# First stage of a spectral GFNet and GEGLU kernel: half of the column table mirrored, angles and statistics moved between engines

## The chip, the cores and the metric

One Trainium2 chip, one core. The metric is the device time of one execution in microseconds (us), median of the runs shown. The engines of the core are TensorE (PE, matrix products; PEld is its weight load), VectorE (DVE), ScalarE (ACT), GpSimd (POOL) and SyncE (SP, whose queue issues DMA transfers). Each engine takes its instructions in the order in which the program lists them and waits where a semaphore is not yet there.

## The reference

Batch 1, S = 2048 rows, D = 576 columns, F = 4608, bf16 inputs:

```python
X = rfft2(layernorm(x).astype(f32), axes=(-2, -1))
y = irfft2(X * (w_r + 1j * w_i), s=(S, D), axes=(-2, -1)).astype(bf16)
h = x + y
h2 = h + (gelu(layernorm(h) @ w_gate) * (layernorm(h) @ w_up)) @ w_down
```

`layernorm` has no weights, `eps` is 1e-5, `gelu` is the tanh form.

## The kernel before

The kernel has two halves: the spectral half (two-dimensional transform, product with the filter, inverse transform), which ends at about 68 us, and the gated feed-forward half, which takes the rest. Nothing in the second half is touched.

**Tiling.** The 2048 rows lie as 128 partitions by 16 tiles h: row 16p + h is in partition p, tile h, in `h_sb`. The row transform is split: first a transform of length 16 over groups of partitions (`row16`, a product with the table `F16`), then the column transform with the table `DT` (`f2`), then the twiddles with the table `TF` (`f3`), the filter (`wmul`), and the inverse with the turned twiddle table `TI` (`i3`) and the turned column table `DQ` (`inv_cols`).

**The first stage** is all that is written between lines 174 and 451, an order laid out by hand: there is no scheduler, each engine gets its instructions in the order of the text. It does this:

- The tables. POOL makes index patterns with `iota` and the rounding of the column phases (`kd`, lines 198 and 199); DVE makes the phases (`phases`, line 268) and drops their sign for the cosine (`drop_sign`, line 223); ACT evaluates the sines of the column table `DT` (`col_sin`, line 347, once for sine, once for cosine, 3 x 290 = 870 elements each). The last slice of the table, `D3`, is copied by DVE into the zeroed `DF` (lines 429 and 430).
- The twiddles `TF`: nine orders k of 128 angles. DVE computes the angle (`angle_a`, line 236), brings it into range (`angle_b`, lines 246 and 247) and drops its sign (`angle_c`, line 223); ACT makes the sine (line 253) and cosine (line 256); DVE negates the sine (`minus_sine`, line 259). This is done for two orders first (`first`), ahead of norms(4,8), and for the seven others (`rest`) after the row transform. `turn_tf` (line 262) has SP issue a transposing transfer of TF into TI, once for `first`, once for `rest`.
- Statistics. Nine tiles by DVE (`sd`, which calls `ln_dve`: two bn_stats and an aggregate, lines 116 to 118), seven by ACT (`ln_act`, line 123: tiles 1, 3, 5, 7, 9, 11, 13), whose sums POOL completes (`ln_fin`). POOL takes the power -0.5 for four tiles at a time (`ln_rstd`, lines 132 and 133).
- `norms(lo, hi)`: DVE normalises a tile (line 136), PE multiplies it (`row16`, line 298, and `row16_rest`, line 311, for the part of the columns that is left over). ACT copies the products from PSUM into `Bt` (`evict`, line 322; `evict4`, line 328, whose last call is on DVE). PSUM has four slots of two banks (`two`), handed out in turn; the next user waits until the slot has been read.
- `fill` (line 286) has PE do products that nobody reads: 14 ahead of tile 0, 8 ahead of tile 8, 5 ahead of tile 12, and 3 ahead of the small product `pt` (line 437), from which ACT makes the table `G16` and its negative (line 445).
- The second halves of the filter tables `WR` and `WI` are mirrored rows: POOL gathers them by an indirect transfer (line 381), SP copies them into place (line 411), POOL halves two columns (line 413).

**The SP queue** behind the loads: WR (copy), WI (copy), first `turn_tf`, thirteen pieces of `DQ` (line 421), second `turn_tf` (issued from the loop below, at i = 2), then the first weights of the feed-forward half (`load_gu`, line 145).

**The second stage** is a software pipeline over eight orders k in the order 1, 2, ..., 7, 0 (lines 668 to 709):

```python
if not last:
    f2(order[i])
    if i != 1: f2_out(order[i])
if i == 0:
    f2(order[0] + 8); angle_c(rest); cosine(rest)
    for r in range(2):
        f2_out(order[0] + 8, V.tensor_copy, slice(r, r + 1))
    minus_sine(rest)
```

`f2` is PE's product with `DT` and `DF` (`pq_ps`, line 479), `f2_out` its copy `pq` (line 490, on ACT, except for the second order's two halves on DVE shown here), `f3` the twiddles (`gh_ps`, lines 496 and 497, copied into `g` at line 518), `sum_of` and `wmul` DVE's sums and filter products (lines 529 to 568), `i3` the inverse (`eo_ps`, line 587). i3 of the third order is the first to read a part of TI that the second `turn_tf` writes.

Of the kernel before, what the change touches and what calls it, by code (L numbers as in the profile page):

```python
# [20 lines left out]
P = 128  # L21
S = 2048
# [7 lines left out]
NFT = F // P  # L30
NR = D // 64
NDT = 5
JW = 58
NW = JP // JW
FQ = 3
# [6 lines left out]
def kernel_body(  # L42
# [23 lines left out]
    def two(name):  # L66
        return psum.tile([P, 2, 512], FP32, name=name, tag="two", bufs=4)
# [115 lines left out]
    iota(kv[:, 0:7], [[1, 7]], 1)  # L183
    iota(kv[:, 7:9], [[8, 2]])
    q16 = tmp("q16", [P, P], FP32)
    iota(q16[:], [[16, P]])
    make_identity(nc, ident[:])
    iD = tmp("iD", [P, 3], FP32)
    iota(iD[:], [[P, 3]], 0, 1)
    iota(iD[64:128, 2:3], [[0, 1]], 2 * P + 64 + 192, 1)  # L190
    iJ = tmp("iJ", [P, JP], FP32)
    iota(iJ[:], [[1, 2], [2, JH]])
    iDs = tmp("iDs", [P, 3], FP32)
    G.tensor_scalar(iDs[:], iD[:], 1.0 / D, None, op0=ALU.mult)
    pd, kd = tmp("pd", [P, 3, JP], FP32), tmp("kd", [P, 3, JP], FP32)
# [16 lines left out]
    ia, s2a, s2p = tmp("ia", [P, 1]), tmp("s2a", [P, 1], FP32), tmp("s2p", [P, 1], FP32)  # L212
    V.tensor_scalar(ia[:], ip[:], 7, None, op0=ALU.bitwise_and)
    V.tensor_scalar(s2a[:], ia[:], 127.0 / 8.0, None, op0=ALU.mult)
    V.scalar_tensor_tensor(s2p[:], ip[:], 0.125, s2a[:], op0=ALU.mult, op1=ALU.add)
    ks = tmp("ks", [P, 9], FP32)
    V.tensor_scalar(ks[:], kv[:], s2p[:, 0:1], None, op0=ALU.mult)
    V.tensor_scalar(iu[:], iu[:], 7, None, op0=ALU.bitwise_and)
    mask = tmp("mask", [P, P], FP32)
    V.tensor_scalar(mask[:], iu[:].rearrange("p c l -> p (c l)"), 0.0, None, op0=ALU.is_equal)  # L220

    def drop_sign(dst, src):
        V.tensor_scalar(
# [10 lines left out]
    def angle_a(sl):  # L234
        n = sl.stop - sl.start
        V.scalar_tensor_tensor(
            pr[:, sl],
            q16[:].unsqueeze(1).to_broadcast([P, n, P]),
            s2p[:, 0:1],
            ks[:, sl].unsqueeze(2).to_broadcast([P, n, P]),  # L240
            op0=ALU.mult,
            op1=ALU.add,
        )

    def angle_b(sl):
        V.tensor_scalar(pr[:, sl], pr[:, sl], 2047, None, op0=ALU.bitwise_and)
# [23 lines left out]
            )  # L270

    def row_table():
        V.tensor_tensor(
            F16[:, 0:2, :],
            fs[:].unsqueeze(1).to_broadcast([P, 2, P]),
            mask[:].unsqueeze(1).to_broadcast([P, 2, P]),
            ALU.mult,
        )
        V.tensor_scalar(F16[:, 2, :], F16[:, 0, :], -1.0, None, op0=ALU.mult)

    ps_f = {}

    def fill(dst, n):

        for _ in range(n):
            T.matmul(dst, lhsT=ident[:], rhs=h_sb[:, 0, 0:512], start=True, stop=True)  # L286

    def row16(h):
        if h % 2 == 0 or h == H - 1:
            ps_f[h] = two("f2t")  # L290
        if h % 4 == 0:
            ps_f["f4", h] = two("f4")
        f2t, b = (ps_f[h], 0) if h in ps_f else (ps_f[h - 1], 1)
        fill(f2t[:, b, :], {0: 14, 8: 8, 12: 5}.get(h, 0))
        x = xn[:, h, :]
        for t in range(2):
            for n, d0 in ((0, t * P), (1, DH + t * P)):
                T.matmul(  # L298
                    f2t[:, b, t * 2 * P : (t + 1) * 2 * P],
                    lhsT=x[:, d0 : d0 + P],  # L300
                    rhs=F16[:, n : n + 2, :],
                    start=(n == 0),
                    stop=(n == 1),
                )
        if h < 12:
            row16_rest(h)

    def row16_rest(h):
        o = (h % 4) * P
# [17 lines left out]
    def evict4(h):  # L327
# [2 lines left out]
            ps_f["f4", h][:, 0].rearrange("p (h c l) -> p h c l", h=4, c=16),  # L330
        )

    def sd(*hs):
        for h in hs:
            ln_dve(mv, h)

    def norms(lo, hi):
        for h in range(lo, hi):
# [1 line left out]
            row16(h)  # L340

    wm = [tmp(n, [P, 8 * J], BF16) for n in ("wm_r", "wm_i")]
    xn_pool = tc.tile_pool(name="xn", bufs=1, side="right")
    xn = xn_pool.__enter__().tile([P, H, D], BF16, name="xn")

    def col_sin(r, src, bias):
        A.activation(  # L347
            DT[:, :, :, r, :],
            src[:].rearrange("p t (a j) -> p t a j", a=2),
            ACT.Sin,  # L350
            bias=bias[:],
            scale=-2.0 * PI / D,
        )

    first, rest = slice(0, 2), slice(2, 9)
    ln_act(1)
    ln_act(3)
    sd(0)
    row_table()
    sd(2)  # L360
    ln_fin(slice(1, 4, 2))
    ln_rstd(rstd, mv, 0, 4)
    sd(4, 6)
    norms(0, 4)
    ln_act(5)
    ln_act(7)
    ln_fin(slice(5, 8, 2))
    ln_rstd(rstd, mv, 4, 8)
    ln_act(9)
    evict(0)  # L370
    ln_act(11)
    evict4(0)
    evict(2)
    angle_a(first)
    angle_b(first)
    angle_c(first)
    sine(first)
    cosine(first)
    norms(4, 8)
    for t, w in zip(wm, (A_w_r, A_w_i)):  # L380
        G.indirect_dma_start(
            out=t[:],
            out_offset=None,
            in_=w.rearrange("(a r) j -> a (r j)", r=8),
            in_offset=bass.IndirectOffsetOnAxis(ap=rev[:, 0:1], axis=0),
        )
    G.memset(DF[:], 0.0)
    ln_fin(slice(9, 12, 2))
    sd(8, 10)
    ln_rstd(rstd, mv, 8, 12)  # L390
    evict(4, 6)
    evict4(4)
    ln_act(13)
    sd(12, 14)
    norms(8, 12)
    sd(15)
    ln_fin(slice(13, 14))
    ln_rstd(rstd, mv, 12, 16)
    for z in Zts:
        G.memset(z[:].rearrange("p a w b j -> p (a w b) j")[:, :, JW:], 0.0)  # L400
    phases()
    drop_sign(kd[:], pd[:])
    evict(8, 10)
    evict4(8)
    col_sin(1, pd, zerob)
    col_sin(0, kd, hpib)
    norms(12, 16)
    minus_sine(first)

    for w, t in ((WR, wm[0]), (WI, wm[1])):  # L410
        nc.sync.dma_start(w[:, 9 : H + 1, 0:J], t[:].rearrange("p (r j) -> p r j", r=8))
    for w in (WR, WI):
        G.tensor_scalar(w[:, :, 0 : J : J - 1], w[:, :, 0 : J : J - 1], 0.5, None, op0=ALU.mult)
    turn_tf(first)
    for r in (1, 0):
        for w in range(1 - r, NW):
            j0, j1 = w * JW, (w + 1) * JW
# [7 lines left out]
    for h in range(12, 16):  # L425
        row16_rest(h)
    evict(12, 14, 15)
    angle_a(rest)
    V.tensor_copy(DF[0:32], D3[0:32])
    V.tensor_copy(DF[96:128], D3[96:128])  # L430
    evict4(12)
    angle_b(rest)
    pt = two("pt")
    fill(pt[:, 1, :], 3)
    for x in range(2):
        for p0 in (0, 64):
# [4 lines left out]
                start=True,  # L441
                stop=True,
            )
    for sign in range(2):
        A.activation(
            G16[:, sign, :, :].rearrange("p x q -> p (x q)"),
            pt[:, 0, 0 : 2 * P],
            ACT.Copy,
            scale=G_SCALE if sign == 0 else -G_SCALE,
        )  # L450
    sine(rest)

    xn_pool.__exit__(None, None, None)
    spw = tc.tile_pool(name="spw", bufs=1)
# [565 lines left out]
```

## Time and profile before

| what | us |
|---|---|
| median of 3 runs | 497.56 (497.55 to 497.57) |
| the profiled execution, its own time | 497.44 |
| its span in the profile | 495.7 |
| PE busy | 487.6 (98%) |
| DVE busy | 224.9 (45%) |
| ACT busy | 161.6 (33%) |
| POOL busy | 29.3 (6%) |
| PE, first product of the second stage (`pq_ps`) starts | 25.2 |
| granted PE clock, in each of the slices | full |

How to read it: the shares are means over the whole span. In the first slices the other engines are as busy as PE or more so: from 8 to 12 us DVE is busy for 3.61 of 4.00 us, ACT for 4.00 and PE for 3.98, of which a part are products that nobody reads. From 28 us on PE is busy without a break. The chain of waits says for each moment what the end hung on; the timelines say what stood in each engine's row.

### The profile page before, as it was taken

Reading aid. Unit: us, or ns where it says so; the run is one execution under the profiler, and the core shown is the slowest. Engines: PE = TensorE matmul, PEld = TensorE weight load, DVE = VectorE, ACT = ScalarE, POOL = GpSimd, SP = SyncE. Lnnn points to the kernel's source line nnn. Section 1 sums busy time; section 2 is a strip of 40 time slices with the busy share of each in tenths; the row PEclk is TensorE's granted clock in tenths of the full one; section 3 lists DMA queues with packets and bytes.
Section 4 is the critical chain, followed back from the end, with each engine's and each line's share of the span. In section 5 each row is a group of like instructions: output and inputs, shape, how many; then the busy total and the mean of one; then the engine's idle time right before and its main releaser. Section 6 shows DMA issues by size and latency. Waiting matters only on the chain.

```text
span 495.7 us, 12763 instructions
## 1 busy us (share of the span) xinstructions
PE 487.6 (98%) x5714; PEld 337.6 (68%) x5716; DVE 224.9 (45%) x443; ACT 161.6 (33%) x289; POOL 29.3 (6%) x78
## 2 busy tenths in 40 slices
PE   6999999999999999999999999999999999999997
PEld 3478789885579965555599855555799655555995
DVE  8999884698632157433311244333221333333111
ACT  8999873322211022323300123223110233232000
POOL 8500010011110001000000000000000000000000
PEclk9999999999999999999999999999999999999999
DMA  8739779969990039988730079977700288870000
GB/s 291 214 52 201 207 148 207 185 107 211 213 210 4 3 84 180 209 166 153 145 73 3 1 177 187 199 153 147 144 3 1 79 156 158 156 149 2 13 15 24
DMA packets 89549, 62.33 MB, mean 126 GB/s; under 512 B 23190, under 2 KB 88086, under 8 KB 89494
## 3 DMA queue, kind: packets, MB, share of 16 engines
q1 hardware_dynamic: 89206, 60.34, 61.5%
q0 software_dynamic: 288, 1.18, 0.8%
q8 instruction: 44, 0.72, 0.7%
q14 instruction: 11, 0.09, 0.1%
HBM read 52.65 MB, written 2.36 MB: 111 GB/s over the span
## 4 chain that ended last, share of the span: by engine, by line
PE 95%; POOL 2%; DVE 1%; ACT 1%; issue 0%; POOLq 0%
PE gu L898 57%; PE acc L941 27%; PE pq_ps L479 2%; PE cs_ps L638 2%; PE acc L960 2%; PE eo_ps L587 2%; PE y_ps L770 1%; PE gh_ps L497 1%; PE gh_ps L496 1%; DVE xn L136 1%; POOL rstd L133 0%; PE f2t L298 0%; ACT DT L347 0%; ACT Bt L322 0%; POOL kd L198 0%
## 5 line engine op out<-in xcount | busy, mean ns | idle before, releaser
L898 PE MATMUL gu<-Bt,wgu 64*128 64x512 bf16 (+1 forms) x2646 | 270.6, 363 | 0.0
L898 PEld LDWEIGHTS <-wgu 64*128 64x128 bf16 x2646 | 151.8, 94 | 115.3 <-issue 0.3
L907 DVE TENSOR_TENSOR P_sb<-g_sb,gu 128x512 bf16<-128x512 f32 (+1 forms) x156 | 100.4, 645 | 140.3 <-ACT g_sb L906 140.3
L906 ACT ACTIVATE g_sb<-gu 128x512 f32<-128x512 f32 (+1 forms) x156 | 88.0, 564 | 193.5 <-PE gu L898 193.5
L941 PEld LDWEIGHTS <-P_sb 64*128 64x128 bf16 x2160 | 122.2, 94 | 10.9
L941 PE MATMUL acc<-wd,P_sb 64*128 64x288 bf16 x1440 | 90.9, 283 | 0.0
L950 DVE TENSOR_TENSOR part<-part,acc 128x576 f32<-128x576 f32 x15 | 11.3, 755 | 112.6 <-ACT part L949 112.6
L949 ACT COPY part<-acc 128x576 f32<-128x576 f32 x15 | 9.6, 640 | 122.8 <-PE acc L941 122.8
L941 PE MATMUL acc<-wd_a,P_sb 64*128 64x288 bf16 x720 | 46.8, 283 | 0.0
L898 PE MATMUL gu<-Bt,wgu_e 64*128 64x256 bf16 (+1 forms) x162 | 12.5, 305 | 0.0
L795 DVE TENSOR_SCALAR hrow<-h_sb,mv,rstd 128x1152 bf16<-128x1152 bf16 x14 | 12.2, 868 | 0.6 <-POOL rstd L833 0.6
L479 PE MATMUL pq_ps<-DT,Bt 128*128 128x290 bf16 x64 | 12.3, 286 | 0.0
L286 PE MATMUL f2t<-h_sb,ident 128*128 128x512 bf16 x26 | 8.3, 473 | 3.9 <-DMA h_sb<-in_A_x_dram 3.9
L133 POOL TENSOR_TENSOR rstd<-rstd,mhalf 128x1 f32<-128x1 f32 (+1 forms) x16 | 11.7, 729 | 1.3
L952 DVE TENSOR_TENSOR h_sb<-h_sb,part 128x576 bf16<-128x576 bf16 x15 | 11.4, 758 | 0.5
L898 PEld LDWEIGHTS <-wgu_e 64*128 64x128 bf16 x162 | 10.4, 94 | 1.1
L479 PEld LDWEIGHTS <-Bt 128*128 128x128 bf16 x96 | 9.2, 97 | 2.5
L132 POOL TENSOR_SCALAR rstd<-mv 128x1 f32<-128x1 f32 (+1 forms) x16 | 4.0, 247 | 116.4 <-DVE mv L118 116.1
L638 PE MATMUL cs_ps<-DQ,EO 58*128 58x290 bf16 x144 | 10.8, 283 | 0.0
L490 ACT CAST pq<-pq_ps 128x580 bf16<-128x580 f32 x15 | 9.9, 663 | 0.2
L298 PE MATMUL f2t<-F,xn 128*128 128x256 bf16 x64 | 9.3, 275 | 0.6 <-DVE xn L136 0.6
L123 ACT ACTIVATE junk<-h_sb 128x576 bf16<-128x576 bf16 x14 | 9.4, 674 | 0.6 <-DMA h_sb<-in_A_x_dram 0.6
(138 smaller groups left out, 280.0 us busy)
## 6 DMA issues: line engine op xcount, KB each, us to landing
wgu<-in_B_w_gate_dram SPq DMA_DIRECT2D x46, 432.0 KB
wgu<-in_B_w_up_dram SPq DMA_DIRECT2D x46, 432.0 KB
wd_a<-in_B_w_down_dram SPq DMA_DIRECT2D x1, 1728.0 KB
wd<-in_B_w_down_dram SPq DMA_DIRECT2D x1, 1728.0 KB
wd<-in_B_w_down_dram SPq DMA_DIRECT2D x6, 288.0 KB
out_dram<-h_sb SPq DMA_DIRECT2D x3, 576.0 KB
h_sb<-in_A_x_dram SPq DMA_DIRECT2D x4, 288.0 KB
h_sb<-in_A_x_dram SPq DMA_DIRECT2D x2, 576.0 KB
```

The costliest lines, as they stand in the source:

```text
L133: G.tensor_tensor(dst[:, sl], dst[:, sl], mhalf[:, sl], ALU.pow)
L479: T.matmul(ps[:, par, 0:JP], lhsT=Bt[:, t, col], rhs=DT[:, t // 2, par] if t < 4 else DF[:, par], start=(t == par), stop=(t == 4),)
L587: T.matmul(pv[:, n], lhsT=z[:, a, w].rearrange("p b j -> p (b j)"), rhs=TI[:, ts[k], 1 - a : 3 - a, :], start=(a == 0), stop=(a == 1),)
L638: T.matmul(ps[:, e, 0:JP], lhsT=EO[x][rows, w, 2 * g : 2 * g + 2].rearrange("p h e k l -> p (h e k l)"), rhs=DQ[rows, w] if w or e else DT ...
L795: V.tensor_scalar(hrow[:], h_sb[:, h, :].rearrange("p (r k) -> p r k", k=64).unsqueeze(2).to_broadcast([P, NR, 2, 64]), mv2[:, h, 0:1], rs ...
L898: T.matmul(gu[:, c, 0:n], lhsT=w[rows, r, i * P : (i + 1) * P], rhs=hl[tcnk % 2][rows, r, lo:hi], start=(r == 0), stop=(r == NR - 1),)
L906: A.activation(g_sb, gu[:, 0, 0:n], ACT.Gelu_apprx_tanh)
L907: V.tensor_tensor(p_sb(f)[:, lo:hi], g_sb, gu[:, 1, 0:n], ALU.mult)
L941: T.matmul(accs[i][:, c, 0:DH], lhsT=p_sb(f)[rows, st * P : (st + 1) * P], rhs=wd[f // NWA][rows, f % NWA, c * DH : (c + 1) * DH], start=( ...
L950: V.tensor_tensor(part, part, accs[1][:, :, 0:DH], ALU.add)
L952: V.tensor_tensor(hv, hv, part, ALU.add)
L960: T.matmul(acc[:, 0, 0:DH], lhsT=p_sb(f)[:, st * P : (st + 1) * P], rhs=wd[f // NWA][:, f % NWA, cc], start=(f == 0), stop=(f == NFT - 1),)
```

## The change

The text of the first stage is rearranged, and some instructions get another form or engine:

- The column table: phases and sines are computed for 73 of the 145 columns of each kind (`JM = 73`), so ACT's two sines have 438 elements each. The others are mirror images with a sign that depends on the partition's parity: a new function `mirror` has DVE write them with four tensor_scalar instructions. The last column of one kind is zeroed by POOL.
- The first two twiddles' angles go to POOL (`first_a`, `first_b`: five instructions), among its statistics; DVE only drops the sign. ACT makes their sines after the last eviction. The other angles keep their form, but `angle_a` and `angle_b` come later in DVE's row, and `angle_c` moves behind the two copies `f2_out(order[0] + 8)`.
- Tile 13's statistics go from ACT to DVE; in `sd` a tile's aggregate is issued between the two bn_stats of the next.
- `gather(1)`, the indirect transfer for WI, is issued by POOL after the last `ln_rstd`; `gather(0)` keeps its place. The memsets of DF, and of the table's last column, follow it.
- The leftover products of four tiles (`rests`) are issued together behind the tiles; fills are 14 ahead of tile 0 and 12 ahead of tile 8, none ahead of tile 12.
- The mask of the row table is folded into one instruction; the negative of `G16` is made by DVE.

Core of the diff:

```diff
-    iJ = tmp("iJ", [P, JP], FP32)
-    iota(iJ[:], [[1, 2], [2, JH]])
+    iJ = tmp("iJ", [P, 2 * JM], FP32)
+    iota(iJ[:], [[1, 2], [2, JM]])
...
+    def first_a():
+        G.tensor_scalar(qs[:, 0], q16[:], s2p[:, 0:1], None, op0=ALU.mult)
+        G.tensor_tensor(
+            prf[:], qs[:].to_broadcast([P, 2, P]), ks[:, 0:2].unsqueeze(2).to_broadcast([P, 2, P]), ALU.add
+        )
+
+    def first_b():
+        G.tensor_scalar(abf[:], prf[:], 1.0 / S, C23, op0=ALU.mult, op1=ALU.add)
+        G.tensor_scalar(abf[:], abf[:], -C23, -float(S), op0=ALU.add, op1=ALU.mult)
+        G.tensor_tensor(prf[:], prf[:], abf[:], ALU.add)
+
+    def first_sines():
+        A.activation(TF[:, 0:2, 2, :], prf[:], ACT.Sin, bias=zerob[:], scale=2.0 * PI / S)
+        A.activation(TF[:, 0:2, 1, :], abf[:], ACT.Sin, bias=hpib[:], scale=-2.0 * PI / S)
...
+    FILL = {0: 14, 8: 12}
...
     def sd(*hs):
         for h in hs:
-            ln_dve(mv, h)
+            st = roll.tile([P, 2, 6], FP32, name="st", tag="st", bufs=3)
+            V.bn_stats(st[:, 0, :], h_sb[:, h, 0:DH])
+            flush()
+            V.bn_stats(st[:, 1, :], h_sb[:, h, DH:D])
+            agg.append((h, st))
...
+    def mirror(r):
+        for a in range(2):
+            V.tensor_scalar(
+                DT[:, :, a, r, JM - a : JH - a], DT[:, :, a, r, JM - 2 :: -1], sgn[:, r : r + 1], None, op0=ALU.mult
+            )
```

The order of the first stage after the change (row table and constants left out):

```python
for h in (1, 3, 5, 7, 9, 11): ln_act(h)
row_table(); sd(0, 2); minus_row(); sd(4)
ln_fin(slice(1, 4, 2)); ln_rstd(rstd, mv, 0, 4)
sd(6); flush(); phases()
norms(0, 4); rests(0)
drop_sign(kd[:], pd[:])
ln_fin(slice(5, 8, 2)); ln_rstd(rstd, mv, 4, 8)
gather(0); evict(0, 2); evict4(0); sd(8)
norms(4, 8); rests(4)
first_a(); sd(10, 12)
ln_fin(slice(9, 12, 2)); ln_rstd(rstd, mv, 8, 12)
col_sin(1, pd, zerob); col_sin(0, kd, hpib)
evict(4, 6); evict4(4)
sd(13, 14, 15); flush(); first_b()
norms(8, 12); ln_rstd(rstd, mv, 12, 16); rests(8)
gather(1); G.memset(DF[:], 0.0); G.memset(DT[:, :, 1, :, JH - 1], 0.0)
norms(12, 16); rests(12)
evict(8, 10); evict4(8)
mirror(1); mirror(0)
V.tensor_copy(DF[0:32], D3[0:32]); V.tensor_copy(DF[96:128], D3[96:128])
drop_sign(abf[:], prf[:])
evict(12, 14, 15); evict4(12)
...
first_sines(); angle_a(rest); minus_sine(first); turn_tf(first)
...
angle_b(rest)
```

And at i = 0 of the second stage:

```diff
             f2(order[0] + 8)
-            angle_c(rest)
-            cosine(rest)
             for r in range(2):
                 f2_out(order[0] + 8, V.tensor_copy, slice(r, r + 1))
+            angle_c(rest)
+            sine(rest)
+            cosine(rest)
             minus_sine(rest)
+            V.tensor_scalar(G16v[1], G16v[0], -1.0, None, op0=ALU.mult)
```

SP's copies of WR and WI into place, and the first `turn_tf` behind them, keep their order in SP's row; `DQ` still comes in thirteen pieces.

More of the change, by code (lines that the diff above doesn't have):

```diff
@@ L32 @@
 NDT = 5
+JM = 73
 JW = 58
@@ L185, in kernel_body @@
     q16 = tmp("q16", [P, P], FP32)
-    iota(q16[:], [[16, P]])
+    iota(q16[:], [[2, P]])
     make_identity(nc, ident[:])
@@ L211, in kernel_body @@
     )
[L212 to L215, printed above, removed]
+    V.tensor_scalar(iu[:], iu[:], 7, None, op0=ALU.bitwise_and)
+    odd, sgn = tmp("odd", [P, 1]), tmp("sgn", [P, 2], FP32)
+    s2p = tmp("s2p", [P, 1], FP32)
+    V.tensor_scalar(odd[:], ip[:], 1, None, op0=ALU.bitwise_and)
+    V.scalar_tensor_tensor(s2p[:], iu[:, 0, 0:1], 127.0, ip[:], op0=ALU.mult, op1=ALU.add)
+    for r, s in ((0, -2.0), (1, 2.0)):
+        V.tensor_scalar(sgn[:, r : r + 1], odd[:], s, -0.5 * s, op0=ALU.mult, op1=ALU.add)
     ks = tmp("ks", [P, 9], FP32)
[L217 to L220, printed above, removed]
+    V.tensor_scalar(ks[:], kv[:], s2p[:, 0:1], 0.125, op0=ALU.mult, op1=ALU.mult)
     def drop_sign(dst, src):
@@ L243, in angle_a @@
         )
+    qs, prf, abf = (tmp(n, [P, w, P], FP32) for n, w in (("qs", 1), ("prf", 2), ("abf", 2)))
+    def first_a():
[10 more added lines that the diff above has]
+        A.activation(TF[:, 0:2, 1, :], abf[:], ACT.Sin, bias=hpib[:], scale=-2.0 * PI / S)
     def angle_b(sl):
@@ L272, in row_table, with minus_row @@
     def row_table():
-        V.tensor_tensor(
+        V.scalar_tensor_tensor(
             F16[:, 0:2, :],
+            iu[:].rearrange("p c l -> p (c l)").unsqueeze(1).to_broadcast([P, 2, P]),
+            0.0,
             fs[:].unsqueeze(1).to_broadcast([P, 2, P]),
-            mask[:].unsqueeze(1).to_broadcast([P, 2, P]),
-            ALU.mult,
+            op0=ALU.is_equal,
+            op1=ALU.mult,
         )
+    def minus_row():
         V.tensor_scalar(F16[:, 2, :], F16[:, 0, :], -1.0, None, op0=ALU.mult)
     ps_f = {}
+    FILL = {0: 14, 8: 12}
     def fill(dst, n):
@@ L290, in row16 @@
             ps_f[h] = two("f2t")
-        if h % 4 == 0:
-            ps_f["f4", h] = two("f4")
         f2t, b = (ps_f[h], 0) if h in ps_f else (ps_f[h - 1], 1)
-        fill(f2t[:, b, :], {0: 14, 8: 8, 12: 5}.get(h, 0))
+        fill(f2t[:, b, :], FILL.get(h, 0))
         x = xn[:, h, :]
@@ L304, in row16, with rests @@
                 )
-        if h < 12:
-            row16_rest(h)
+    def rests(h):
+        ps_f["f4", h] = two("f4")
+        for i in range(4):
+            row16_rest(h + i)
     def row16_rest(h):
@@ L331, in evict4, with flush @@
         )
+    agg = []
+    def flush():
+        while agg:
+            h, st = agg.pop()
+            V.bn_aggr(mv[:, h, :], st[:])
     def sd(*hs):
         for h in hs:
-            ln_dve(mv, h)
+            st = roll.tile([P, 2, 6], FP32, name="st", tag="st", bufs=3)
[3 more added lines that the diff above has]
+            agg.append((h, st))
     def norms(lo, hi):
@@ L342, in kernel_body, with gather @@
     wm = [tmp(n, [P, 8 * J], BF16) for n in ("wm_r", "wm_i")]
+    def gather(i):
+        G.indirect_dma_start(
+            out=wm[i][:],
+            out_offset=None,
+            in_=(A_w_r, A_w_i)[i].rearrange("(a r) j -> a (r j)", r=8),
+            in_offset=bass.IndirectOffsetOnAxis(ap=rev[:, 0:1], axis=0),
+        )
     xn_pool = tc.tile_pool(name="xn", bufs=1, side="right")
@@ L347, in col_sin @@
         A.activation(
-            DT[:, :, :, r, :],
+            DT[:, :, :, r, 0:JM],
             src[:].rearrange("p t (a j) -> p t a j", a=2),
@@ L353, in col_sin @@
         )
+    def mirror(r):
+        for a in range(2):
+            V.tensor_scalar(
+                DT[:, :, a, r, JM - a : JH - a], DT[:, :, a, r, JM - 2 :: -1], sgn[:, r : r + 1], None, op0=ALU.mult
+            )
     first, rest = slice(0, 2), slice(2, 9)
-    ln_act(1)
-    ln_act(3)
-    sd(0)
+    for h in (1, 3, 5, 7, 9, 11):
+        ln_act(h)
     row_table()
-    sd(2)
+    sd(0, 2)
+    minus_row()
+    sd(4)
     ln_fin(slice(1, 4, 2))
     ln_rstd(rstd, mv, 0, 4)
-    sd(4, 6)
+    sd(6)
@@ L364, in kernel_body @@
+    flush()
+    phases()
     norms(0, 4)
-    ln_act(5)
-    ln_act(7)
+    rests(0)
+    drop_sign(kd[:], pd[:])
     ln_fin(slice(5, 8, 2))
     ln_rstd(rstd, mv, 4, 8)
-    ln_act(9)
-    evict(0)
-    ln_act(11)
+    gather(0)
+    evict(0, 2)
     evict4(0)
[L373 to L378, printed above, removed]
-    norms(4, 8)
[L380 to L386, printed above, removed]
@@ L387, in kernel_body @@
-    G.memset(DF[:], 0.0)
+    sd(8)
+    norms(4, 8)
+    rests(4)
+    first_a()
+    sd(10, 12)
     ln_fin(slice(9, 12, 2))
-    sd(8, 10)
     ln_rstd(rstd, mv, 8, 12)
+    col_sin(1, pd, zerob)
+    col_sin(0, kd, hpib)
     evict(4, 6)
     evict4(4)
-    ln_act(13)
-    sd(12, 14)
+    sd(13, 14, 15)
+    flush()
+    first_b()
     norms(8, 12)
-    sd(15)
-    ln_fin(slice(13, 14))
     ln_rstd(rstd, mv, 12, 16)
+    rests(8)
+    gather(1)
+    G.memset(DF[:], 0.0)
+    G.memset(DT[:, :, 1, :, JH - 1], 0.0)
@@ L399, in kernel_body @@
+    norms(12, 16)
+    rests(12)
+    evict(8, 10)
+    evict4(8)
+    mirror(1)
+    mirror(0)
+    V.tensor_copy(DF[0:32], D3[0:32])
+    V.tensor_copy(DF[96:128], D3[96:128])
+    drop_sign(abf[:], prf[:])
+    evict(12, 14, 15)
+    evict4(12)
     for z in Zts:
         G.memset(z[:].rearrange("p a w b j -> p (a w b) j")[:, :, JW:], 0.0)
[L401 to L408, printed above, removed]
@@ L410, in kernel_body @@
     for w, t in ((WR, wm[0]), (WI, wm[1])):
         nc.sync.dma_start(w[:, 9 : H + 1, 0:J], t[:].rearrange("p (r j) -> p r j", r=8))
+    first_sines()
+    angle_a(rest)
+    minus_sine(first)
+    turn_tf(first)
     for w in (WR, WI):
         G.tensor_scalar(w[:, :, 0 : J : J - 1], w[:, :, 0 : J : J - 1], 0.5, None, op0=ALU.mult)
-    turn_tf(first)
     for r in (1, 0):
@@ L423, in kernel_body @@
                     )
[L425 to L432, printed above, removed]
     pt = two("pt")
@@ L443, in kernel_body @@
             )
[L444 to L451, printed above, removed]
+    G16v = [G16[:, sign].rearrange("p x q -> p (x q)") for sign in range(2)]
+    A.activation(G16v[0], pt[:, 0, 0 : 2 * P], ACT.Copy, scale=G_SCALE)
+    angle_b(rest)
     xn_pool.__exit__(None, None, None)
```

2 lines of the change are left out of this document (1 added, 1 removed).

## The prediction

> **What bounds the kernel now.** I read the page first, then the chain of waits in order of time, then the timelines of VectorE (DVE), GpSimd (POOL), ScalarE (ACT) and the DMA queue (SP) up to 42 us.
>
> The page gives TensorE (PE) 98% of the span, and the chain that ended last names it for 95%. The rest is the first stage. In the chain (start, length, what) it ends so:
>
> ```profile
> 16.74 0.31 DVE xn L136
> 17.09 0.61 PE f2t L298 x4
> ...
> 19.90 1.01 ACT Bt L322
> 20.97 0.31 issue
> 21.28 1.95 ACT DT L347 x2
> 23.23 0.91 ACT Bt L322
> 24.18 0.38 PE pt L286
> ...
> 25.22 2.34 PE pq_ps L479 x18
> ...
> 41.62 1.09 PE eo_ps L587 x10
> ```
>
> ACT sets the end of the first stage: two eviction copies, the two sines of the column table (L347), then the last copies to 25.10 us. From 25.16 us to the end I find no PE start that is late by more than 0.3 us. So a stretch taken from the front shortens the kernel only if PE then stays fed, and any later stall is paid in full.
>
> The three queues that PE depends on right behind that point (columns: start, length, engine, line, operation):
>
> ```profile
> 23.94 0.43 DVE L430 COPY DF<-DT 32x580 bf16<-32x580 bf16 x1
> 24.40 0.69 DVE L328 CAST Bt<-f 128x512 bf16<-128x512 f32 x1
> 25.12 0.63 DVE L246 TENSOR_SCALAR pr<-pr 128x896 int32<-128x896 int32 x1
> ...
> 26.45 0.63 DVE L223 TENSOR_SCALAR ab<-ab 128x896 int32<-128x896 int32 x1
> 26.99 0.82 DVE L490 CAST pq<-pq_ps 128x290 bf16<-128x290 f32 x2
> ```
>
> ```profile
> 27.26 1.06 ACT L256 ACTIVATE TF<-ab,nhpib 128x896 bf16<-128x896 f32 x1
> 28.20 0.65 ACT L518 CAST g<-gh_ps 128x578 bf16<-128x578 f32 x1
> ```
>
> ```profile
> 18.66 0.61 SPq L411 DMA_DIRECT2D WI<-wm_i  x1
> 22.72 1.32 SPq L262 DMA_TRANSPOSE TI<-TF  x1
> 24.14 9.87 SPq L421 DMA_DIRECT2D DQ<-DT  x13
> 34.12 3.62 SPq L262 DMA_TRANSPOSE TI<-TF  x1
> ```
>
> DVE has work without a hole from 8.6 to 28 us, and the late angles feed the cosine on ACT, behind which the copy of g waits. SP is a strict row: first turn of TF, thirteen pieces of DQ at about 0.76 us each, second turn of TF. The trace's landing marks put that second turn at 39.85 us; the first matmul that reads it, i3 of the third order, starts at 41.45 us. Margin: 1.6 us.
>
> **The change, part by part,** on before's clock.
>
> *Statistics on DVE.* A tile took 0.93 us (13.88 to 14.80); 0.48 of it is the second bn_stats and the wait of the aggregate for it. With another tile's bn_stats in between this wait (about 0.11, against the spacing of 0.37 between two bn_stats) goes: 0.81 a tile. Between norms(4,8), which still end at 12.90 because ACT's sums of tile 7 set their rstd, and norms(8,12) there are now five tiles instead of four: 5 x 0.81 + 0.3 = 4.35, so 17.25 instead of 16.66. Tile 13's 1.34 us leave ACT (17.20 to 18.54). The phases (1.33 for 290 columns, some 0.75 for 146) move into the slack ahead of norms(0,4), where DVE waited only 0.18 but gains 0.5 by the interleaving: nothing.
>
> *POOL.* Its row becomes: gather(0) at 11.55 (1.25 long), first_a, rstd of 8 to 11, first_b, rstd of 12 to 15, then gather(1). A tensor_scalar of 290 took 0.52 and one of 870 took 0.93, so 256 cost about 0.5 and 128 about 0.4. A two-input add of 256 elements is not in the trace: not below 0.45 (the scalar form), not above 0.93 (the 870 row); I take 0.65. So 12.85 + 1.1 = 13.95; sums 0.56; wait for tile 10's mean to 14.55; 0.32 + pow 1.05 = 15.95; first_b 0.52 + 0.52 + 0.65 + gaps = 17.75; rstd 0.3 + pow 1.24 to 1.38 (what it took beside normalising or phases) = 19.4. Hence norms(12,16) run from 19.4 to 20.8 instead of 21.00 to 22.44, 1.6 earlier, and gather(1) starts at 19.45 instead of 13.13.
>
> The Trainium skill, GPSIMD Engine Reference, "4.1 Engine selection", speaks against these adds: two-input elementwise work belongs on VectorE and is about twice as slow here. Its "2.1 Instruction dispatch" has a floor of 2.5 cycles an element, and "1. Specifications" a clock of 1.2 GHz: an estimate of 0.53 us for 256, and with 0.53 in both adds POOL would be 0.24 earlier than in my row. No row of before shows it.
>
> *ACT and the start of PE's second stage.* The sines of the column table are half as wide (0.92 for 870 and 0.41 for 256 give 0.56 for 438) and run at about 14 to 15 us, while ACT waits for rows 8 and 9 anyway. PE does rows 8 to 15 from 17.7 to 21.65 and the rests to 21.9. ACT copies back to back from 19.8: 0.89 + 0.47 + 0.89 + 0.48 + 0.48, ending at 23.1 instead of 25.10. First pq_ps at 23.2: 1.95 us earlier. The fewer fills (26 instead of 27 ahead of rows, placed at rows 0 and 8) lie in PE's waits: row 8's twelve run from 14.3 to 16.9, its data comes at 17.7.
>
> *DVE behind norms(12,16): here the gain is given back.* From 20.8: four mirror instructions of 216 elements. None is in the trace; between 0.14 (L259's spacing, 256 bf16) and 0.33 (L247's spacing, 256 fp32): the mirrors step backwards and take a factor per partition, so I take the middle, 0.23, and 0.9 for four, bounds 0.55 to 1.3; 21.7. DF copies 0.77; 22.5. Sign of the first angles 0.33; 22.8. evict4(12) 0.72; 23.5. angle_a of the late angles 1.07; 24.6. minus_sine 0.14, landing at 24.95. angle_b 0.66 + 0.54; 25.95. The two pq copies 0.74; 26.7, where PE, through with its 18 pq_ps matmuls at 25.5, has waited a microsecond for them. Only then angle_c, done at 27.35. The cosine stands ahead of the copy of g on ACT: 27.35 + 0.95 = 28.3, before 28.20. What follows (pq, f3 of the second order) hangs on g's place in ACT's row, and has before's timing to 0.1 us. So the 1.95 us buy nothing: the end shifts by +0.1, with the bounds of mirrors and POOL by -0.5 to +0.9.
>
> *SP.* WI's second half waits for gather(1). The gathers landed 4.70 and 5.52 after their start, the second behind the first's data; alone I take 4.7: 24.15. Its issue takes 0.66, to 24.8. turn_tf(first), which is queued behind it and also waits for minus_sine, goes at 25.0 instead of 22.72: +2.3. Nothing in the row behind it is shorter: DQ still thirteen pieces, second turn issued at 36.4, landed at 39.85 + 2.3 = 42.15. i3 of the third order then starts at 42.2 instead of 41.45: **+0.75 us**, and no PE slack follows. With 5.5 for the gather it is +1.35; with everything early, +0.1. The front's +0.1 is hidden inside this stall, it does not add. POOL's 0.5 on WI, due at 29.6, and the m memsets behind it come out just ahead of the first product (30.40). The weights of the second half load 2.3 us later; the first is wanted only at 68 us and had landed by 45, so that costs nothing.
>
> *Moved off:* the second copy of G16 (0.28 on ACT) to DVE's wait at 27.9; minus_row and the rest tables of TF, each in a wait.
>
> Sum against the profiled execution (497.44 us, span 495.7; 1.74 around it; median of the runs 497.56): +0.8 gives 498.24 to 498.36. I say **498.3**.
>
> **Rivals.**
> 1. *Slower by over 0.2%.* Place: POOL's row from 12.85 to 19.4. If the two adds or the pows take 0.3 each more, or the gather lands after 5.5, the second turn lands past 42.5; from there the stall is over 1.0. At the upper bounds (adds 0.93, gather 5.5) +1.4 + 0.55 = about 499.4. For: every step of POOL is in series and gather(1) is last. Against: DMA is idle after 21 us, so 4.7 is the likelier landing. Mean 499.0.
> 2. *The second turn is not late.* If rstd of 12 to 15 comes by 18.8 (adds at 0.45) and the gather lands after 4.4, the turn lands by 41.5, and the front decides: -0.5 to +0.2, about 497.4. For: the margin of 1.6. Against: minus_sine alone, at 24.95, uses it up.
> 3. *The start's gain arrives.* If mirrors cost 0.14 and POOL is 0.5 early, DVE's chain ends about a microsecond before mine, and the turn with it: 496.4. Against: SP would need turn_tf by 23.5, with three late steps all at their lower bound.
>
> **How the numbers follow.** About 0.2%, 1.0 us here, is what a measurement of this kernel can tell from no change. Forecast (+0.1 to +1.0) 0.45; rival 1 0.32; rival 2 0.16; rival 3 0.07. Rival 2 and the forecast are within 0.2%: about 0.6, with a little of rival 1's near end; slower 0.32; faster 0.07. The range takes the forecast, most of rival 2 and rival 1 up to +1.7: 497.3 to 499.2.
>
> **What would show it.** Right: first pq_ps near 23.2; a PE hole of about 1 us before f3 of the first order, ended by DVE's pq copy; the cosine of the late angles starting as angle_c ends, g near 28.3; turn_tf(first) near 25; PE waiting some 0.75 us before an eo_ps near 41.4, ended by the second turn of TF. Wrong: no PE wait at that eo_ps; gather(1) before 18.5 or after 20; pq copies on DVE before 26 us.

## The result, and the profile after

| | median, us | range, us | runs |
|---|---|---|---|
| before | 497.55 | 497.31 to 498.08 | 7 |
| after | 499.10 | 498.98 to 499.35 | 7 |

The ratio is 1.0032, with a 95% interval of 1.002 to 1.0043: the change makes the kernel 1.55 us slower. The profiled execution after took 498.99 us with a span of 497.2 us, 1.5 us longer than the span before, and the granted PE clock is full in both.

The chain of waits of the kernel after, in order of time (start, length, engine, what, line):

```profile
18.36 1.05 POOL rstd L134
19.43 3.16 DVE xn L137 x4
...
25.01 1.06 DVE pr L237
...
27.41 0.73 DVE pq L531 x2
...
28.71 1.04 ACT TF L274
29.75 0.53 ACT g L559
...
43.01 1.25 PE eo_ps L628 x10
```

Before, this chain ran over ACT's evictions and sines. Now it runs from POOL's last pow over the last four normalises (`xn`, line 137) and the whole of DVE's row to the copies of pq, then over ACT's cosine (line 274) to the copy of g. The second entry is the new one: four normalises take 3.16 us. In the kernel before the same four took 1.52 us, with the Zt memsets beside the first of them (start, length, engine, line, operation, count):

```profile
21.00 1.52 DVE L136 TENSOR_SCALAR xn<-h_sb,mv,rstd 128x576 bf16<-128x576 bf16 x4
```

```profile
20.70 0.64 POOL L400 MEMSET Zt<- 128x120 bf16 x3
```

DVE's and POOL's timelines of the kernel after at this place (in brackets the idle time before an entry and what ended it):

```profile
17.00 1.81 DVE L137 TENSOR_SCALAR xn<-h_sb,mv,rstd 128x576 bf16<-128x576 bf16 x4
19.43 3.16 DVE L137 TENSOR_SCALAR xn<-h_sb,mv,rstd 128x576 bf16<-128x576 bf16 x4 [0.62 <-POOL rstd L134]
22.51 0.87 DVE L404 TENSOR_SCALAR DT<-DT,sgn 128x216 bf16<-128x216 bf16 x4
...
27.32 0.82 DVE L531 CAST pq<-pq_ps 128x290 bf16<-128x290 f32 x2
```

```profile
17.09 0.87 POOL L257 TENSOR_TENSOR prf<-prf,abf 128x256 f32<-128x256 f32 x1
...
19.58 1.12 POOL L382 DMA_INDIRECT wm_i<-in_A_w_i_dram,rev  x1 [0.18 <-issue]
20.71 0.59 POOL L446 MEMSET DF<- 128x580 bf16 x1
...
21.27 0.48 POOL L460 MEMSET Zt<- 128x120 bf16 x3
```

The single instructions behind the 3.16 us are 0.49, 2.08, 0.41 and 0.42 us long. The second, that of tile 13, starts at 19.84 and ends at 21.92, 0.17 after POOL's last Zt memset (21.75). In the group of 17.00, tile 9 takes 0.83 instead of 0.42 and ends at 18.13, 0.17 after POOL's two-input add (17.96).

PE's row has two waits that it did not have before:

```profile
27.83 0.28 PE L538 MATMUL gh_ps<-pq,TF 128*128 128x289 bf16 x1 [0.59 <-DVE pq L531]
30.33 0.41 PE L520 MATMUL pq_ps<-DT,Bt 128*128 128x290 bf16 x2 [0.74 <-ACT g L559]
```

And SP's row:

```profile
24.20 0.61 SPq L462 DMA_DIRECT2D WI<-wm_i  x1
26.28 1.36 SPq L280 DMA_TRANSPOSE TI<-TF  x1
27.73 9.80 SPq L475 DMA_DIRECT2D DQ<-DT  x13
37.66 3.35 SPq L280 DMA_TRANSPOSE TI<-TF  x1
```

The first pq_ps product starts at 24.72, only 0.43 us earlier than before. With the two waits the products behind it are late: the second product of the second order's f3, which I take as the mark of the front, starts at 31.42 instead of 30.05 (+1.37). i3 of the third order, where the second turn of TF is wanted, starts at 43.01 instead of 41.45 (+1.56), and the end is +1.55 late. So 1.4 us are lost at the front and about 0.2 at the turn. The two marks in PE's row, before and after:

```profile
30.05 0.28 PE L497 MATMUL gh_ps<-pq,TF 128*128 128x289 bf16 x1
...
41.45 1.25 PE L587 MATMUL eo_ps<-TI,Zt 128*128 128x256 bf16 x10
```

```profile
31.42 0.28 PE L538 MATMUL gh_ps<-pq,TF 128*128 128x289 bf16 x1
...
43.01 1.25 PE L628 MATMUL eo_ps<-TI,Zt 128*128 128x256 bf16 x10
```

### The profile page after: what moved, and what is told of

Read it like the earlier page. It is cut to its first block, busy times and chain, and to the rows that moved or that the text cites. A ratio compares the mean times of both kernels' runs of the same rounds, so it can differ in the third digit from the quotient of the medians.

```text
span 497.2 us, 12763 instructions
## 1 busy us (share of the span) xinstructions
PE 485.7 (98%) x5715; PEld 337.4 (68%) x5715; DVE 225.4 (45%) x448; ACT 159.4 (32%) x284; POOL 31.4 (6%) x82
## 4 chain that ended last, share of the span: by engine, by line
PE 93%; DVE 2%; POOL 2%; ACT 1%; issue 1%; DMA 1%; POOLq 0%; DVEq 0%
PE gu L941 56%; PE acc L984 27%; PE cs_ps L679 2%; PE acc L1003 2%; PE eo_ps L628 2%; PE pq_ps L520 2%; PE y_ps L813 1%; ACT junk L124 1%; PE gh_ps L538 1%; POOL rstd L134 1%; PE gh_ps L537 1%; DVE xn L137 1%; DMA h_sb<-in_A_x_dram 1%; POOL wm_r L382 0%; PE eo_ps L652 0%
## 5 line engine op out<-in xcount | busy, mean ns | idle before, releaser
L319 PE MATMUL f2t<-F,xn 128*128 128x256 bf16 x64 | 8.1, 273 | 3.2 <-DVE xn L137 3.1
L319 PEld LDWEIGHTS <-xn 128*128 128x128 bf16 x64 | 5.8, 98 | 5.8 <-DVE xn L137 4.9
```

Source lines behind the costliest of these rows:

```text
L319: T.matmul(f2t[:, b, t * 2 * P : (t + 1) * 2 * P], lhsT=x[:, d0 : d0 + P], rhs=F16[:, n : n + 2, :], start=(n == 0), stop=(n == 1),)
```

## The experiments

Three theories. **A:** POOL's instructions beside them hold DVE's normalises, and this sets the end. **B:** SP's row decides, as the prediction had it: the second turn of TF comes late for i3 of the third order. **C:** DVE's and ACT's rows behind the normalises (late angles, pq, cosine, g) give back what the start gains, hold or no hold.

This table holds the profiled execution of each kernel: when the last four normalises run, and how far the first pq_ps product, the front, the third order's i3 and the end stand from the kernel before (us).

| kernel | last four xn | first pq_ps | front | third i3 | end | median |
|---|---|---|---|---|---|---|
| before | 21.00 to 22.52 | 0 | 0 | 0 | 0 | 497.55 |
| after | 19.43 to 22.59 | -0.43 | +1.37 | +1.56 | +1.55 | 499.10 |
| b1_late_gather | 20.90 to 23.25 | +0.63 | +0.62 | +2.19 | +2.19 | 499.61 |
| b2_mirror_alone | 20.75 to 22.31 | -0.62 | +0.55 | +0.55 | +0.55 | 498.14 |
| e1_gather_early | 20.23 to 22.35 | -0.58 | +1.13 | +1.23 | +1.21 | 498.91 |
| e2_memsets_away | 19.54 to 21.26 | -1.85 | -0.03 | +1.09 | +1.09 | 498.57 |
| e3_both | 20.41 to 21.87 | -1.07 | +0.90 | +0.87 | +0.85 | 498.45 |
| e4_both_dq_late | 20.32 to 21.80 | -1.13 | +0.54 | +0.52 | +0.55 | 498.84 |
| e9_memsets_dq | 19.39 to 21.11 | -1.56 | -0.17 | -0.20 | +0.15 | 497.48 |
| e5_rstd_first | 19.42 to 22.16 | -1.04 | +0.89 | +1.11 | +1.10 | 498.21 |
| e6_best | 18.96 to 21.71 | -1.50 | -0.22 | -0.25 | -0.25 | 497.24 |
| e7_clear | 19.91 to 21.36 | -1.48 | -0.47 | -0.57 | -0.53 | 496.92 |
| e8_one_memset | 19.90 to 21.57 | -1.35 | -0.19 | -0.29 | -0.24 | 497.20 |
| e10_cosine_last | 20.08 to 21.52 | -1.41 | -1.06 | -0.40 | -0.18 | 497.62 |

The kernel before ran beside each of them: its median was 497.55 beside e1 to e6, b1 and b2, 497.66 beside e7 to e9 and 497.46 beside e10. Ratios are to that median, with a 95% interval.

**The gather back to its old place (e1), the memsets away (e2), both (e3).** Edits of the kernel after:

```diff
     gather(0)
+    gather(1)
...
     rests(8)
-    gather(1)
```

```diff
     iota(rev[:], [[0, 1]], 2 * P - 1, -2)
+    G.memset(DF[:], 0.0)
+    G.memset(DT[:, :, 1, :, JH - 1], 0.0)
...
     gather(1)
-    G.memset(DF[:], 0.0)
-    G.memset(DT[:, :, 1, :, JH - 1], 0.0)
...
     for m in (m1, m2):
         G.memset(m[:, :, :, J:], 0.0)
+    for z in Zts:
+        G.memset(z[:].rearrange("p a w b j -> p (a w b) j")[:, :, JW:], 0.0)
```

In the second, the Zt memsets go from behind `evict4(12)` to this place.

> The changed kernel with gather(1) issued right behind gather(0), as in the kernel before; the memsets of DF, of the table's last column and of the Zt tiles stay behind the last pow. Theory A-gather (the issue of the transfer holds DVE's normalise beside it): the normalise of tile 13 goes from 2.08 us back to 0.42 to 0.5, norms(12,16) take 1.4 to 1.6 us instead of 3.1, and the front (first f3 of the third order) comes about 1.3 us earlier. Theory A-memset (POOL's memsets hold it): POOL's memsets now stand right behind the pow, so one or two of the four normalises still take over 1 us and norms(12,16) stay near 3.1 us. Theory B (the queue of SP decides as predicted): the first turn of TF no longer waits for WI, goes at the end of minus_sine, about 24.7 to 26.2 us, and the time is 498.0 to 498.5. Time by A-gather 497.6 to 498.3 (the second turn of TF is late next), by A-memset about 499.0.

> The changed kernel with the memsets of DF and of the table's last column moved to the table stage and those of the Zt tiles behind the memsets of m; gather(1) stays behind the last pow. Theory A-gather: one normalise of the last four still ends only when POOL's issue of the transfer ends (about 20.7 us), so norms(12,16) take about 2.1 us; time about 498.2 to 498.6. Theory A-memset: all four take 0.42 to 0.45, norms(12,16) take 1.4 us from 19.4, time 497.8 to 498.3. If neither holds DVE, norms(12,16) stay at 3.1 us and the time at 499.1.

> Both edits: gather(1) right behind gather(0), all memsets away from the last normalises. Theory A: norms(12,16) take 1.4 us from 19.4, the front moves up by 1.3 to 1.7 us, to -0.3 to +0.1 against the kernel before. Then theory B: the second turn of TF, issued behind the thirteen pieces of DQ, lands at 41.5 to 42.1 and i3 of the third order waits for it; time 498.0 to 498.3, +0.5 to +0.7 against the kernel before. Theory C (DVE's late angles and the copies of pq give the gain back, without any hold by POOL): norms(12,16) at 1.4 us but the front still at +0.8 or more, time 498.5 to 499.1.

Ratios to before: 1.0033 (1.0021 to 1.0045), 1.0021 (1.0011 to 1.0031), 1.0019 (1.001 to 1.0028). In e1 the memsets now meet the first normalise, which takes 1.10 and ends 0.16 after the last of them. In e2 the four take 0.48, 0.42, 0.62 and 0.43, the 0.62 beside the end of the gather's issue. In e3 all four take 0.42 to 0.43. So the memsets are the larger holder and the gather's issue the smaller. The parts do not add: against the 1.45 us of four normalises with nothing beside them (e7, below) the memsets alone cost 0.7, the gather alone 0.3, both together 1.7. Theory A holds for the normalises; for the time it does not hold alone, as e2 shows. In time e1 (498.65 to 499.87) can't be told from the kernel after (498.98 to 499.35), nor e3 from e2; only the rows of the traces tell them apart. PE's and SP's timelines of e2:

```profile
23.31 0.67 PE L520 MATMUL pq_ps<-DT,Bt 128*128 128x290 bf16 x4
...
26.43 0.28 PE L538 MATMUL gh_ps<-pq,TF 128*128 128x289 bf16 x1 [0.60 <-DVE pq L531]
...
28.94 0.41 PE L520 MATMUL pq_ps<-DT,Bt 128*128 128x290 bf16 x2 [0.73 <-ACT g L559]
...
42.55 1.25 PE L628 MATMUL eo_ps<-TI,Zt 128*128 128x256 bf16 x10 [0.98 <-DMA TI<-TF]
```

```profile
24.29 0.61 SPq L460 DMA_DIRECT2D WI<-wm_i  x1
25.00 2.02 SPq L282 DMA_TRANSPOSE TI<-TF  x1
```

With the memsets away PE begins 1.85 us earlier than before. It loses all of it again: about 0.8 and 0.9 us at the two waits for DVE's pq and ACT's g, and 0.2 just ahead of the front's product (theory C). Then it waits 0.98 us for the second turn of TF (theory B). The last normalise ends 1.3 us earlier than in the kernel after, but the time falls by only 0.5, because B stands right behind it. e3 misses its expected front (+0.90, not -0.3 to +0.1): gather(1) ahead of two pows delays the last one (done at 20.38 in e3 and 20.20 in e1, against 19.40 in the kernel after), and POOL's halving of WI and the Zt memsets now meet `angle_b`, whose first step takes 0.82 instead of 0.62.

**DQ behind the second turn, on e3 (e4).** The thirteen DQ transfers go behind `turn_tf(rest)`.

> As the run with both edits, and the thirteen pieces of DQ behind the second turn of TF in SP's row. Theory B: the second turn now lands about 33 to 35 us, i3 of the third order no longer waits for it, and what is left is the front's shift of -0.3 to +0.1: time 497.3 to 497.7, 0.5 to 0.7 below the run with both edits. If the second turn of TF costs nothing (theory A or C alone), the time is that of the run with both edits within 0.2 us. DQ lands later, near 45 us; its first reader is the inverse column transform, behind the second stage, so no stall is expected from it.

1.0026 (1.0016 to 1.0036), 498.84. It could not show B: in e3 the late front already covers the turn, no i3 waits for it. Its runs also scatter from 498.02 to 499.39, the profiled one being the lowest; what the others wait for was not seen.

**DQ split around the second turn, on e2 (e9).** This asks the same where the front is early:

```diff
+    turn_dt(1)            # the seven DQ pieces of r = 1
...
                     turn_tf(rest)
+                    turn_dt(0)            # the six of r = 0
```

> The run with the memsets away, with one thing more: seven pieces of DQ ahead of the second turn of TF in SP's row and six behind it. Theory B: the wait of 0.99 us ahead of i3 of the third order goes, because the second turn lands near 37 instead of 42.5; only the front's shift of about 0 is left, so the time falls by 0.9 to 1.1 us to 497.5 to 497.8. If SP's row were not what holds that i3, the time stays at 498.57.

0.9995 (0.9986 to 1.0004), 497.48: 1.1 us less than e2, while the kernel before, beside e9, was 0.1 higher than beside e2. PE's row at that i3, without a wait:

```profile
41.13 0.28 PE L522 MATMUL pq_ps<-DF,Bt 128*128 128x290 bf16 x1
41.26 1.25 PE L630 MATMUL eo_ps<-TI,Zt 128*128 128x256 bf16 x10
```

So B is shown, at about 1.1 us where the front is not late. The second turn was issued at 33.25 and landed 6.6 us later, at 39.9 and not near 37 as expected; that is still 1.4 us ahead of i3. Between that i3 and the end e9 loses 0.35 us again, at an inverse column product near 60 us; its cause was not followed.

**One part of the change alone, in the kernel before (b1, b2).**

```diff
     ln_rstd(rstd, mv, 12, 16)
+    gather(1)
+    G.memset(DF[:], 0.0)
     for z in Zts:
```

```diff
     norms(12, 16)
+    mirror(1)
+    mirror(0)
     minus_sine(first)
```

In b1 both are taken from behind gather(0). b2 also has the tables 73 columns wide, `sgn`, and the zeroed last column, as in the change.

> The kernel before with one part of the change alone: gather(1) and the memset of DF go behind the last pow, the Zt memsets follow them as before. Theory A (POOL's issue and memsets hold DVE's normalise): one of the last four normalises takes about 2 us, norms(12,16) take about 3.1 us instead of 1.44, and the first pq_ps product comes 1.2 to 1.7 us late. Theory B (SP's row): WI's copy goes at about 26 us and the first turn of TF at about 26.6 instead of 22.72, so the second turn lands near 43.7 and i3 of the third order starts there instead of at 41.45. The two overlap, so the end moves by the larger: by B 499.6 to 500.0, by A alone 498.8 to 499.2. If the late gather is harmless, 497.6.

> The kernel before with the half column table alone: ACT's two sines have 438 elements each, DVE's four mirrors stand between norms(12,16) and minus_sine. If ACT's evictions set the front, as the chain of waits says, the last one ends about 0.7 us earlier and the time falls to about 496.9. Theory C (DVE's row from the normalises to the pq copies sets it as soon as ACT is faster): the mirrors take 0.81 us, the pq copies start near 27.8 instead of 26.99, PE waits some 0.8 us before an f3 of the first order, and the time is 498.1 to 498.4. The first turn of TF goes 0.8 later and still lands ahead of i3 of the third order, so theory B adds nothing.

b1: 1.0041 (1.0025 to 1.0056). PE's row and DVE's normalises in it:

```profile
43.65 1.25 PE L591 MATMUL eo_ps<-TI,Zt 128*128 128x256 bf16 x10 [1.42 <-DMA TI<-TF]
```

```profile
20.90 2.36 DVE L136 TENSOR_SCALAR xn<-h_sb,mv,rstd 128x576 bf16<-128x576 bf16 x4
```

B gives the time within its bounds, +2.19. A's 3.1 us was too much: here the normalises take turns with POOL (0.43, 0.90, 0.76, 0.51), and POOL's memsets are longer too (DF 0.72 instead of 0.60). Of the two parts tried alone this is by far the dearer.

b2: 1.0011 (1.0002 to 1.002), +0.6 us. ACT's last eviction is earlier and PE begins 0.62 us sooner, but the front is 0.55 late. DVE's row:

```profile
22.23 0.87 DVE L362 TENSOR_SCALAR DT<-DT,sgn 128x216 bf16<-128x216 bf16 x4
...
27.56 0.82 DVE L504 CAST pq<-pq_ps 128x290 bf16<-128x290 f32 x2
```

The pq copies start 0.57 later than before (26.99), and everything behind them is late by that. The chain of waits of the kernel before named ACT; but DVE's first pq copy there ended at 27.44, 0.1 us ahead of the f3 product at 27.55, so DVE's row took over at once. This is theory C by itself.

**Putting the parts right (e5, e6, e7, e10), and one memset put back (e8).** e5: e3 with first_b and the Zt memsets behind the last pow. e6: e5 with DQ split, `angle_a(rest)` ahead of `evict4(12)`, and on ACT the copies of g and of the second order's pq ahead of the cosine. e7 keeps e6's DQ split and its order on ACT and takes POOL's work away from the last eight normalises, all but first_b's two scalar steps:

```diff
-        G.tensor_tensor(prf[:], prf[:], abf[:], ALU.add)
+    V.tensor_tensor(prf[:], prf[:], abf[:], ALU.add)      # behind the DF copies
...
     first_a()
+    gather(1)
...
+        V.memset(z[:].rearrange("p a w b j -> p (a w b) j")[:, :, JW:], 0.0)   # ahead of norms(4, 8)
...
     evict4(12)
+    angle_a(rest)
```

and has DVE halve WR and WI, and the second step of `angle_b` behind the pq copies. e8 is e7 with `G.memset(DF[:], 0.0)` once more behind the last pow. e10 is e7 with gather(1) behind first_b's two steps, and the cosine behind the second order's second pq copy.

> As the run with both edits, and first_b behind the last pow instead of ahead of it, with the Zt memsets behind it. POOL's last pow ends at about 18.6 us instead of 20.4, norms(12,16) run from 18.7. Theory A: the two-input add of first_b beside them costs one normalise about 0.4 us and no more. Theory C: PE runs from the first row of tile 8 to the first f3 without a hole, but the cosine still stands ahead of g on ACT, so PE waits about 0.7 us for g; the front is at -0.4. Theory B: the first turn of TF goes near 24.5, the second lands near 41.6, i3 of the third order is about 0.2 later than before: 497.6 to 497.9. If none of the three theories were the cause, the time would stay at that of the run with both edits, 498.45.

> As the run with first_b behind the last pow, and all that theories B and C name taken away: the late angles' first step goes ahead of DVE's last eviction, so the pq copies come at about 25.1; on ACT the copy of g and that of the second order's pq go ahead of the cosine of the late angles; on SP seven pieces of DQ go ahead of the second turn of TF and six behind it, so that it lands near 36 us. Theories A to C together: no PE hole over 0.4 us between 17.6 and 45 us, end 1.0 to 1.6 us earlier than the kernel before, 496.0 to 496.6. If something that none of them names holds the time, it stays above 497.3.

> A version against all three theories: as the last version, and nothing of POOL's runs beside the last eight normalises (the add of first_b, the Zt memsets and the halving of WR and WI on DVE, gather(1) between first_a and the sums); DVE's last eviction ahead of the late angles, and the pq copies between the two steps of angle_b. Theory A: the last eight normalises take 0.42 us each, norms(12,16) run from about 19.0 to 20.4. Theory C: no hole ahead of the first f3, the front 1.2 to 1.6 us earlier than in the kernel before. Theory B: the second turn lands by 37. Time 495.9 to 496.5; over 497.0 means that a fourth cause holds the second stage.

> The version against all three theories with one instruction more: a second memset of DF (128 x 580, about 0.57 us on POOL) right behind the last pow, that is beside norms(12,16). Theory A in its sharper form, from the runs so far (a normalise that runs beside a POOL instruction ends 0.16 to 0.18 us after it): one of the four normalises ends 0.17 us after the memset, takes 0.6 to 0.9 us, and norms(12,16) take 0.3 to 0.5 us longer. PE's rows shift by as much, the end by 0 to 0.4. If memset and normalise don't meet, all four take 0.42 and nothing moves.

> The version against all three theories, with its two remaining holes taken away: gather(1) goes behind first_b's two scalar steps instead of ahead of the sums, so the pow of tiles 8 to 11 ends before DVE is through with the statistics; and the cosine of the late angles goes behind the second copy of the second order's pq on ACT, since TF's rest is read only from the third order on. PE's first row of tile 8 starts near 17.6 instead of 18.18, its wait of 0.6 us before the second order's f3 goes down to 0.2 or less, and the front comes 0.7 to 1.1 us earlier than in that version: 495.8 to 496.3. gather(1) beside a normalise of tiles 8 to 11 costs at most 0.3 us. If the copies on ACT are not what PE waits for there, only the 0.3 to 0.5 us of the start arrive: 496.4 to 496.6.

Ratios: e5 1.0011 (1.0002 to 1.002), e6 0.9994 (0.9985 to 1.0003), e7 0.9986 (0.9977 to 0.9995), e8 0.9989 (0.998 to 0.9998), e10 1.0004 (0.9995 to 1.0013). e5 and e6 miss their forecasts. first_b and the Zt memsets now stand exactly beside the last four normalises: tile 14 takes 1.30 in both and ends 0.16 after the last memset. In e5 the last pow was also done only at 19.39, not near 18.6. e7 and e8 differ by one POOL instruction. DVE's row of e7, then DVE's and POOL's of e8:

```profile
19.91 1.45 DVE L137 TENSOR_SCALAR xn<-h_sb,mv,rstd 128x576 bf16<-128x576 bf16 x4 [0.63 <-POOL rstd L134]
```

```profile
19.90 1.68 DVE L137 TENSOR_SCALAR xn<-h_sb,mv,rstd 128x576 bf16<-128x576 bf16 x4 [0.63 <-POOL rstd L134]
```

```profile
19.81 0.59 POOL L448 MEMSET DF<- 128x580 bf16 x1
```

Tile 12 takes 0.66 instead of 0.43 and ends at 20.56, 0.16 after the memset; the four take 0.23 longer, the front moves by 0.28 and the end of the profiled execution by 0.29 (median of 11 runs each 0.28; their ranges overlap, 496.64 to 497.38 and 496.95 to 497.41). That is theory A with nothing else changed.

e7 is the best kernel of the study, 0.7 us below the kernel before that ran beside it (497.66), but it misses its forecast. Its trace shows three reasons: the last four normalises start at 19.91, not near 19.0, as gather(1) (1.01 us) now stands ahead of both pows in POOL's row; POOL's scalar steps run beside tiles 8 and 9 (0.62 and 0.57); and on ACT the cosine stands ahead of the next pq copy:

```profile
29.57 0.28 PE L538 MATMUL gh_ps<-pq,TF 128*128 128x289 bf16 x1 [0.62 <-ACT pq L531]
```

e10 takes that wait away (front -1.06), yet 0.7 us of it is gone already at the first i3 (-0.37), spread over waits of at most 0.2 us each. gather(1) still stands ahead of the last pow there, and the last four normalises start no earlier (20.08). e10's runs scatter from 497.05 to 498.52; where the longer ones lose time stays open.

## Why the prediction was right in its range and wrong in its forecast

499.10 lies in the range, at its far end. The forecast (+0.1 to +1.0) did not come; the time is that of the side of rival 1, but not by its mechanism: POOL's row was on time and the gather did not land late. That the range holds 499.10 is therefore luck: its far end was there for a late gather, and what came was a hold that the prediction had not priced.

- *Statistics, 0.81 a tile:* measured 0.79; norms(8,12) at 17.00 instead of 17.25. Right.
- *POOL's row:* last pow done at 19.40, gather(1) at 19.58 and landed at 24.18, against 19.4, 19.45 and 24.15. The add taken as 0.65 was 0.61 with only bn_stats beside it and 0.87 beside normalises. Right.
- *norms(12,16) from 19.4 to 20.8:* **this step failed.** I took 4 x 0.34 from before, where nothing of POOL's ran beside them but the Zt memsets, and in the same paragraph put gather(1) at 19.45, with the memsets behind it. Measured 3.16 instead of about 1.4. The sign of it was in the trace of before: its tile 12 takes 0.51 beside the Zt memsets, the others 0.41 and 0.42. e8 shows the effect by itself, e2 what it costs here: 1.4 us of PE's start and 1.4 us of the front.
- *Everything behind it*, counted from where the normalises end: four mirrors 0.81 (taken 0.9), pq copies 4.81 us after the normalises (taken 5.15). In e2, where the last four normalises run nearly as predicted (19.54 to 21.26), the first pq_ps is at 23.31 (predicted 23.2), pq at 25.93 (25.95), g at 28.26 (28.3), the front at -0.03 (+0.1). Right there, and 1.3 to 1.4 late in the kernel after.
- *SP:* turn_tf(first) at 25.00 in e2, as predicted, but the turn then took 2.02 us instead of 1.32, so DQ started at 27.12, the second turn was issued at 37.16 instead of 36.4, and i3 of the third order started at 42.55 instead of 42.2: the stall is +1.09, not +0.75. That term was too small by 0.35, and nothing in the trace of before showed the reason (last section). In the kernel after, turn_tf(first) went only at 26.28, behind the late minus_sine (25.99): the hold moved the turn too.
- *The sum as a maximum, not an addition:* right. In the kernel after the front is 1.37 late and i3, waiting for the turn, 1.56; they do not add, and the end is 1.55 late.
- *The signs named beforehand:* the hole ahead of f3 of the first order, ended by DVE's pq, came (0.59 us instead of about 1), and the cosine started as angle_c ended (28.71). The first pq_ps (24.72), turn_tf(first) (26.28) and g (29.66) came 1.3 to 1.5 us behind the times named, and the stall at i3 was about 0.2 us instead of 0.75.

On the step that failed, the Trainium skill, SBUF — State Buffer, "SBUF: two separate sides" and "Who interferes with whom", says that VectorE and GpSimd share one pair of ports under an exclusive lock: a VectorE instruction in a mode that uses two ports, and tensor_scalar can be one, waits in full for a GpSimd instruction that came first. The rows agree, with an end 0.16 to 0.17 us behind POOL's in e1, e3, e5, e8 and after, and in b1 POOL's DF memset is longer in its turn (0.72 us). In which mode these normalises ran, no run shows. The lock as stated is held for one instruction; that tile 13 waited through the gather's issue and five memsets goes beyond it, and no run here tells why.

## What to carry to other kernels

Moving work to an idle engine is free only if that engine's instructions do not hold the critical one: before a POOL instruction is placed, read which DVE instructions run beside it, and price them at POOL's end, not at their own length. A chain of waits names one row; look also at which other row ends within a few tenths of it, since that one takes over the moment the first is shortened (b2). Where several lateness terms meet at one consumer, curing the largest only uncovers the next: here one cure (e2) ended the normalises 1.3 us earlier and brought 0.5, and the two that belong together (e9) brought 1.6.

## What the runs showed of the hardware

- A POOL memset of 0.59 us beside the first of four normalises makes the four 0.23 us longer and the kernel 0.28 to 0.29 us slower (e8 against e7). bn_stats is not held: 0.40 to 0.44 beside POOL's scalar steps as elsewhere.
- The hold depends on what meets what: in the kernel before, four normalises beside the whole issue of a gather (11.59 to 12.84) take 0.42 to 0.43 each; in the kernel after, two of the four beside the same transfer's issue (11.42 to 12.79) take 0.54 and 0.50; in e2 only the one at the end of the issue of gather(1) takes 0.62. Why the first four go free is open.
- The issue of a transposing transfer 0.10 to 0.35 us behind the copy of WI takes 1.93 to 2.04 us (e2, e9, e10, b1), and 1.32 to 1.36 where 1.4 us or more lie between them (the other ten kernels). The 0.6 to 0.7 us go straight into what is queued behind it. No run varies the pause by itself, so the cause stays open.
- DVE tensor_scalars that read 216 bf16 elements backwards follow each other every 0.20 us (after, e2, b2).
